# Attention and two MLPs on one core: tiles at multiples of 64 bytes, another rhythm of weight conversion, and the last cosine chunk in alternation with the last product

## The chip, the core and the metric

The kernel runs on one core of a Trainium2 chip. The metric is the device time of one execution in microseconds. The kernel before took 1944.91 us, the median of 3 runs (1944.83 to 1947.69).

## What is computed

All inputs are float32 or float64 arrays; the weights come as 64-bit words, which the kernel itself turns into float32.

```python
def _attn_ref(q, k, v):                        # (8, 8, 576, 64) each
    k_p = k.reshape(B, H, Sp, pool, D).mean(axis=3)      # pool = 8: 72 keys
    v_p = v.reshape(B, H, Sp, pool, D).mean(axis=3)
    scores = scale * np.matmul(q, k_p.transpose(0, 1, 3, 2))
    attn = softmax(scores)
    return np.matmul(attn, v_p)
...
x = attn_out.transpose(0, 2, 1, 3).reshape(4608, 512)
x = (sigmoid(x @ w_gate) * (x @ w_val)) @ w_out          # w_gate, w_val 512 x 1536, w_out 1536 x 512
h = x @ w_in                                             # 512 x 2048
out = (h * np.cos(h)) @ w2_out                           # 2048 x 512
```

## The kernel before

**Tiling.** The 4608 tokens make 9 chunks (`NC`) of 512 columns, kept transposed: a tile holds 128 features in its partitions and 512 tokens along them. Each product is made of three: an operand is split into a high part in float32r and the rest, and high x high, high x rest and rest x high are added up in a PSUM bank. So a block of 128 output features over 512 inputs takes 12 matmuls of 128x512 (`group` in what follows): 4 blocks of the contraction, 3 matmuls each. The last product, `y_step`, has the tokens as stationary and the weights as moving operand, and its groups have 12 matmuls too (4 token tiles, 3 each).

**Stages.** First, attention of chunk c + 1 runs beside the gate and value products of chunk c (`gv_step`, 12 pairs of groups `pg`, `pv` a chunk); the gated result goes to DRAM (`gd`). Chunk 8 has no attention beside it; there, from pair 3 on, one group of the product with `w_out` of chunk 0 (`o_step`, `po`) follows each pair, and the three that are left follow the last pair. Then come the cosine products: for each chunk 16 groups `ph` (`h_step`), with the 12 `po` groups of the next chunk between them. One group `ph` with what goes with it is called a turn here. Its cosine takes three operations of VectorE (`n`, `r`, `r`, L485 to L491), two of ScalarE (Sin, Square), and a fourth of VectorE (`rest`, L498), which is held back by one turn; `r` goes to DRAM (`hd`). At last, `y_step` runs 16 groups for each chunk, with `hd` fetched again.

**Order.** The program stands in the order in which it is written; each engine takes its instructions in that order. `o_ahead` and `y_ahead` fetch up to four tiles ahead on SyncE's queue and make the two parts of the next two (`parts`: a cast on ScalarE, a subtraction on VectorE, L66). Of the three matmuls of each contraction block, the first needs the cast and the second the subtraction.

**Weights.** A block of weights is 512 KB. `load_all` fills slots of 4096 bytes a partition; a block's raw words stand two slots ahead of where its parts go. There are 28 slots at first; slots come free as `w_gate`, `w_val` and `w_out` are used for the last time, and six more (`e0` to `e5`) with the pool `hp_`, when the gate stage's tiles are given up. `split` converts in three stages, for two blocks a call: `stage_exponent` (ScalarE, up to four blocks ahead), `stage_bits` (VectorE, two operations a block, L132 and L137), `stage_parts` (cast and subtraction). In chunks 0, 7 and 8 of the cosine products each turn calls `split`; the blocks of `w2_out` from the fifth on are loaded in chunk 7, each as a `w_out` block comes free.

**Banks.** PSUM has 8 banks in two sets of four, `t` and `g`. `pg`, `pv` and `ph` use `g`, attention and `po` use `t`, and chunk c of `y_step` uses `g` for even c, `t` for odd. A `ph` can only start once the `rest` of the fourth one before it is done.

**Addresses.** In the kernel as built, the pool of weights begins at byte 1152 of a partition and every slot in it, as every tile of `mp` behind it (`x2`, `fetch`, `parts`), begins at a multiple of 64. `mask` takes 32 bytes; all of attention's tiles after it begin 32 bytes past a multiple of 64. So does what is laid out from the top of memory, which ends at 229344: the gate stage's `xT` (186336 and 202720) and later `e0` to `e5` (184288 to 208864), where blocks 0 to 5 of `w2_out` end up. The moving operand of the gate stage's matmuls is `xT`, that of `y_step` is the block of `w2_out`, that of `po` and `ph` stands in `mp`.

Of the kernel before, what the change touches and what calls it, by code (L numbers as in the profile page):

```python
# [9 lines left out]
F32 = mybir.dt.float32  # L10
# [13 lines left out]
def attention_two_mlps(  # L24
# [22 lines left out]
    nc = tc.nc  # L47
    B, H, S, D = q.shape
    NT, DM = out.shape
    FF = w_gate.shape[1]  # L50
    FF2 = w2_in.shape[1]
    P = 128
# [5 lines left out]
    NF = FF // P  # L58
    NF2 = FF2 // P
    C = 512  # L60
    NC = NT // C
# [8 lines left out]
    dp = ctx.enter_context(tc.tile_pool(name="dp", bufs=1, space=bass.MemoryType.DRAM))  # L70
    ps = ctx.enter_context(tc.tile_pool(name="ps", bufs=1, space=bass.MemoryType.PSUM))
    at = tc.alloc_tile_pool(name="at", bufs=1, side="left")
    gv = tc.alloc_tile_pool(name="gv", bufs=1, side="right")

    gd = [dp.tile([NF, P, C], F32, name=f"gd{c}") for c in range(NC)]
# [2 lines left out]
    def bank(tag, shape, name):  # L78
        return ps.tile(shape, F32, tag=tag, name=name, bufs=4)
# [18 lines left out]
    slots = [(wp, f"w{n}") for n in range(NSLOT)]  # L98
# [43 lines left out]
    def stage_parts(n):  # L142
        (kind, f), (pool, tag) = order[n], slots[n]
        t = pool.tile([P, 2, 512], F32R, tag=tag, name=f"w{kind}{f}")
        x = words(n, F32, 1)
        nc.scalar.copy(t[:, 0], x)  # L146
        split_lo(nc.vector, t[:, 1], x, t[:, 0])
        blocks[kind, f] = t
        place[kind, f] = slots[n]

    def split(upto=None):

        upto = len(raws) if upto is None else upto
        while done["parts"] < done["bits"]:
            stage_parts(done["parts"])
            done["parts"] += 1
        while done["exponent"] < min(done["bits"] + 4, upto):
            stage_exponent(done["exponent"])
            done["exponent"] += 1
        some = range(done["bits"], min(done["bits"] + 2, done["exponent"]))  # L160
        stage_bits(some)
        done["bits"] += len(some)
# [7 lines left out]


    ident = at.tile([P, P], F32, name="ident")
    mask = at.tile([P, H], F32, name="mask")
    kbds = [at.tile([P, NP, 2 * KEYS], F32, name=f"kbd{n}") for n in range(2)]
    vm = at.tile([P, 2, NP, P], F32R, name="vm")
    vr = at.tile([P, 2, NP, P], F32R, name="vr")
# [274 lines left out]
    graw, gp, po = {}, {}, {}  # L451
# [52 lines left out]
    def y_step(c, j, g):  # L504
        w = block("o2", j)
        wh, wl = w[:, 0], w[:, 1]
        if j == 0:
            po[c] = [bank("gt"[c % 2], [P, DM], f"py{c}_{n}") for n in range(4)]
        for n in range(4):
            p = po[c][n]  # L510
            s = slice(n * P, (n + 1) * P)
            nc.tensor.matmul(p, g[:, 0, s], wh, start=j == 0, stop=False)  # L512
            nc.tensor.matmul(p, g[:, 0, s], wl, start=False, stop=False)  # L513
            nc.tensor.matmul(p, g[:, 1, s], wh, start=False, stop=j == NF2 - 1)  # L514
            if j == NF2 - 1:
                y = hp_.tile([P, DM], F32, tag="y", name=f"y{c}_{n}", bufs=4)
                if n % 2:
                    nc.scalar.mul(y, p, -1.0)
                else:
                    nc.vector.tensor_scalar(  # L520
                        out=y, in0=p, scalar1=-1.0, scalar2=None, op0=ALU.mult
                    )
                nc.sync.dma_start(out[c * C + n * P:c * C + (n + 1) * P, :], y)

    with tc.manual_schedule():
# [38 lines left out]
        at_o = {"fetched": 0, "split": 0, "next": 0}  # L564

        def o_ahead():
            while at_o["fetched"] < min(at_o["next"] + 4, len(osteps)):
                c, f = osteps[at_o["fetched"]]
                graw[c, f] = fetch(gd, c, f, "graw")
                at_o["fetched"] += 1  # L570
            while at_o["split"] < min(at_o["next"] + 2, len(osteps)):
                g_parts(*osteps[at_o["split"]])
                at_o["split"] += 1

        def o_next():
            c, f = osteps[at_o["next"]]
            o_step(c, f)
            at_o["next"] += 1
            if c == NC - 1:
                slots.append(place["o", f])  # L580
                load_all()

        store = None
        for c in range(NC):
            last = c == NC - 1
            beside = [] if last else plan(c + 1)
            if last:
                at.release()
                mp = tc.alloc_tile_pool(name="mp", bufs=1, side="left", reuse_waits="tile")
            for f in range(NF):  # L590
                if last and f >= 2:
                    o_ahead()
                done_ = gv_step(c, f)
                if c == 0:
                    split()
                    for _ in range(2):
                        if len(raws) < len(slots) - AHEAD:
                            load()
                if last:
                    slots.extend(place[kind, f] for kind in "gv")  # L600
                    load_all()
                    split(len(raws) - 2)
                    if f >= 3:
                        o_next()
                elif f % 4 == 3:
                    split()
                if beside:
                    for step in beside[f]:
                        step()
                if store:  # L610
                    store()
                store = done_
# [2 lines left out]

        gv.release()
        hp_ = tc.alloc_tile_pool(name="hp", bufs=1, side="right", reuse_waits="tile")
        slots.extend((hp_, f"e{n}") for n in range(6))
        load_all()
        while at_o["next"] < NF:  # L620
            o_ahead()
            o_next()
            split()

        ys = [(c, j) for c in range(NC) for j in range(NF2)]
        hraw, hp = {}, {}
        at_y = {"fetched": 0, "split": 0}

        def y_ahead(n):
            while at_y["fetched"] < min(n + 4, len(ys)):  # L630
                c, j = ys[at_y["fetched"]]
                hraw[c, j] = fetch(hd, c, j, "hraw")
                at_y["fetched"] += 1
            while at_y["split"] < min(n + 2, len(ys)):
                c, j = ys[at_y["split"]]
                hp[c, j] = parts(hraw.pop((c, j)), f"hp{c}_{j}")
                at_y["split"] += 1

        late = []
        for c in range(NC):  # L640
            for j in range(NF2):
                if c + 1 < NC:
                    o_ahead()
                elif j >= NF:
                    y_ahead(0)
                late.append(h_step(c, j))
                if len(late) > 1:
                    late.pop(0)()
                if c + 1 < NC and j < NF:
                    o_next()  # L650
                if c == 0 or c >= NC - 2:
                    split()
        for fn in late:
            fn()


        for n, (c, j) in enumerate(ys):
            y_ahead(n + 1)
            y_step(c, j, hp.pop((c, j)))
        mp.release()  # L660
        hp_.release()

# [31 lines left out]
```

## Time and profile before

| | |
|---|---|
| median of 3 runs | 1944.91 us |
| the profiled execution | 1945.53 us |
| its span | 1943.8 us |
| TensorE busy | 1863.7 us (96%) |
| VectorE, ScalarE busy | 1018.2 us (52%), 705.4 us (36%) |
| granted clock of TensorE, mean of the span | 0.982 |

The span runs from the first to the last instruction. A matmul of 512 columns is shown with some 0.39 us, though the next one starts earlier: the pitch is read from the starts. The timeline gives start, duration, engine, line, operation and tiles of each instruction and, in brackets, how long its engine had been idle and what ended that. Lines beginning with SPq are issues of DMAs by SyncE.

### The profile page before, as it was taken

How to read it: one execution, taken by the hardware profiler on the slowest of the kernel's cores; microseconds unless marked ns; L12 is line 12 of the kernel's file. 1: busy time of each engine (PE TensorE's matmuls, PEld its weight loads, DVE VectorE, ACT ScalarE, POOL GpSimd, SP SyncE). 2: the span in 40 equal slices, each digit the busy share in tenths (PEclk: the TensorE clock that was granted, in tenths of full speed). 3: DMA queues.
4: the chain of work that ended last, by engine and by line, in shares of the span. 5: the costliest groups of instructions: out<-in, count | busy, mean ns of one | idle time of the engine just before them, and what ended most of it. 6: DMA issues, size and time to landing. Idle time of an engine off the chain costs nothing.

```text
span 1943.8 us, 22603 instructions
## 1 busy us (share of the span) xinstructions
PE 1863.7 (96%) x8384; PEld 1518.7 (78%) x8384; DVE 1018.2 (52%) x1849; ACT 705.4 (36%) x1201; POOL 104.4 (5%) x149
## 2 busy tenths in 40 slices
PE   4899999999999999989999999999878899999999
PEld 3678888888888788878888888888756688888887
DVE  7784353434434344577676676776657722222222
ACT  3563343434334333444333333333334422222222
POOL 3202112021110000000000000000000000000000
PEclk7999999999999999999999999999988999999999
DMA  9533224142241116632322222223332333333333
GB/s 237 173 97 93 80 70 112 42 113 74 77 109 41 55 38 201 194 136 98 99 97 97 98 98 98 97 98 98 105 117 87 133 117 120 115 119 120 114 108 109
DMA packets 151470, 208.06 MB, mean 107 GB/s; under 512 B 48448, under 2 KB 68928, under 8 KB 151360
## 3 DMA queue, kind: packets, MB, share of 16 engines
q1 hardware_dynamic: 151360, 206.62, 34.6%
q8 instruction: 66, 1.08, 0.2%
q14 instruction: 44, 0.36, 0.1%
HBM read 131.07 MB, written 75.50 MB: 106 GB/s over the span
## 4 chain that ended last, share of the span: by engine, by line
PE 85%; DVE 7%; DMA 3%; ACT 2%; issue 1%; SPq 1%; ACTq 0%; DVEq 0%
PE py L514 7%; PE py L512 7%; PE py L513 7%; PE ph L481 5%; PE ph L480 5%; PE ph L482 5%; PE pg L384 5%; PE pg L386 5%; PE pg L385 5%; PE pv L386 5%; PE pv L384 5%; PE pv L385 5%; PE po L467 4%; PE po L466 4%; PE po L468 4%; PE px L371 3%
## 5 line engine op out<-in xcount | busy, mean ns | idle before, releaser
L391 DVE TENSOR_TENSOR g<-pv,s 128x512 f32<-128x512 f32 x108 | 74.6, 691 | 329.8 <-PE pv L386 204.9
L480 PE MATMUL ph<-x,wi 128*128 128x512 f32 x576 | 226.5, 393 | 11.8 <-DVE r L498 11.1
L66 DVE TENSOR_TENSOR hp<-hraw,hp 128x512 fp32r<-128x512 f32 x144 | 98.8, 692 | 259.1 <-ACT hp L442 258.9
L494 ACT ACTIVATE r<-r 128x512 f32<-128x512 f32 x144 | 91.1, 632 | 394.8 <-DVE r L491 394.8
L512 PE MATMUL py<-wo,hp 128*128 128x512 f32 x576 | 225.3, 391 | 1.9 <-DVE r L498 1.9
L481 PE MATMUL ph<-x,wi 128*128 128x512 f32 x576 | 225.9, 392 | 0.3 <-DVE x L66 0.3
L514 PE MATMUL py<-wo,hp 128*128 128x512 f32 x576 | 226.1, 392 | 0.0
L482 PE MATMUL ph<-x,wi 128*128 128x512 f32 x576 | 225.5, 391 | 0.0
L513 PE MATMUL py<-wo,hp 128*128 128x512 f32 x576 | 225.4, 391 | 0.0
L466 PE MATMUL po<-gp,wo 128*128 128x512 f32 x432 | 172.5, 399 | 20.5 <-ACT gp L442 20.5
L442 ACT CAST hp<-hraw 128x512 fp32r<-128x512 f32 x144 | 88.6, 621 | 258.2 <-PE py L514 232.1
L384 PE MATMUL pg<-xT,wg 128*128 128x512 f32 x432 | 179.0, 414 | 0.4 <-ACT wg L146 0.4
L467 PE MATMUL po<-gp,wo 128*128 128x512 f32 x432 | 173.6, 402 | 2.8 <-DVE gp L66 2.8
L386 PE MATMUL pg<-xT,wg 128*128 128x512 f32 x432 | 171.8, 398 | 0.5 <-DVE wg L66 0.4
L385 PE MATMUL pg<-xT,wg 128*128 128x512 f32 x432 | 171.5, 397 | 0.0
L468 PE MATMUL po<-gp,wo 128*128 128x512 f32 x432 | 171.4, 397 | 0.0
L386 PE MATMUL pv<-xT,wv 128*128 128x512 f32 x432 | 170.8, 395 | 0.0
L384 PE MATMUL pv<-xT,wv 128*128 128x512 f32 x432 | 170.7, 395 | 0.0
L385 PE MATMUL pv<-xT,wv 128*128 128x512 f32 x432 | 170.3, 394 | 0.0
L480 PEld LDWEIGHTS ph<-x,wi 128*128 128x128 f32 x576 | 109.0, 189 | 36.6 <-DVE r L498 12.4
L389 ACT ACTIVATE s<-pg 128x512 f32<-128x512 f32 x108 | 64.6, 598 | 190.5 <-PE pg L386 190.1
L66 DVE TENSOR_TENSOR gp<-graw,gp 128x512 fp32r<-128x512 f32 x108 | 74.5, 690 | 105.7 <-ACT gp L442 105.7
(108 smaller groups left out, 3027.2 us busy)
## 6 DMA issues: line engine op xcount, KB each, us to landing
hd<-r SPq DMA_DIRECT2D x144, 256.0 KB
hraw<-hd SPq DMA_DIRECT2D x144, 256.0 KB
gd<-g SPq DMA_DIRECT2D x108, 256.0 KB
graw<-gd SPq DMA_DIRECT2D x108, 256.0 KB
raw_o<-in_moe_w_out_dram SPq DMA_DIRECT2D x28, 512.0 KB
out_dram<-y SPq DMA_DIRECT2D x36, 256.0 KB
raw_k<-in_k_dram SPq DMA_DIRECT2D x32, 256.0 KB
q<-in_q_dram SPq DMA_DIRECT2D x32, 256.0 KB
```

Of the source, the lines that this page charges most:

```text
L384: nc.tensor.matmul(p, wh, x[:, 0, kb], start=kb == 0, stop=False)
L385: nc.tensor.matmul(p, wh, x[:, 1, kb], start=False, stop=False)
L386: nc.tensor.matmul(p, wl, x[:, 0, kb], start=False, stop=kb == KB - 1)
L466: nc.tensor.matmul(p, wh, g[:, 0], start=f == 0, stop=False)
L467: nc.tensor.matmul(p, wh, g[:, 1], start=False, stop=False)
L468: nc.tensor.matmul(p, wl, g[:, 0], start=False, stop=f == NF - 1)
L480: nc.tensor.matmul(p, wh, x[:, 0, kb], start=kb == 0, stop=False)
L481: nc.tensor.matmul(p, wh, x[:, 1, kb], start=False, stop=False)
L482: nc.tensor.matmul(p, wl, x[:, 0, kb], start=False, stop=kb == KB - 1)
L512: nc.tensor.matmul(p, g[:, 0, s], wh, start=j == 0, stop=False)
L513: nc.tensor.matmul(p, g[:, 0, s], wl, start=False, stop=False)
L514: nc.tensor.matmul(p, g[:, 1, s], wh, start=False, stop=j == NF2 - 1)
```

## The change

Four edits:

- **Addresses.** A tile of 32 bytes is allocated at the top of memory, and `mask` is widened to 64 bytes. As built, every operand of every matmul then begins at a multiple of 64: `xT` at 186304 and 202688, `e0` to `e9` at 176064 to 212928.
- **First products of chunk 0.** In the last gate chunk the pairs 3 to 10 are followed by 1, 1, 1, 2, 2, 2, 2 and 1 groups `po`, all twelve, and the loop behind the stage is gone. `hp_` brings ten slots in place of six, so that ten blocks (the last two of `w_in`, the first eight of `w2_out`) are loaded there at once. The output tile `y` shares four buffers with `r`.
- **Conversion.** In chunk 0 each turn calls `split` as before, in all others every third.
- **Last chunk.** In chunk 8 of the cosine products each turn ends with one group of the last product's chunk 0 and `y_ahead`; its first tiles are fetched from turn 12 of chunk 7 on. The last product's bank sets change places. Its other 8 chunks follow.

```diff
+    edge = ctx.enter_context(tc.tile_pool(name="edge", bufs=1, side="right"))
+    nc.gpsimd.memset(edge.tile([P, 8], F32, name="edge"), 0.0)
...
-    mask = at.tile([P, H], F32, name="mask")
+    mask = at.tile([P, 2 * H], F32, name="mask")[:, :H]
...
-            po[c] = [bank("gt"[c % 2], [P, DM], f"py{c}_{n}") for n in range(4)]
+            po[c] = [bank("tg"[c % 2], [P, DM], f"py{c}_{n}") for n in range(4)]
...
-                y = hp_.tile([P, DM], F32, tag="y", name=f"y{c}_{n}", bufs=4)
+                y = hp_.tile([P, DM], F32, tag="r", name=f"y{c}_{n}", bufs=4)
...
-                    if f >= 3:
+                    for n in range((0, 0, 0, 1, 1, 1, 2, 2, 2, 2, 1, 0)[f]):
+                        if n:
+                            o_ahead()
                         o_next()
...
-        slots.extend((hp_, f"e{n}") for n in range(6))
+        slots.extend((hp_, f"e{n}") for n in range(10))
         load_all()
-        while at_o["next"] < NF:
-            o_ahead()
-            o_next()
-            split()
...
             for j in range(NF2):
-                if c + 1 < NC:
+                if not last:
                     o_ahead()
-                elif j >= NF:
-                    y_ahead(0)
+                    if c == NC - 2 and j >= NF:
+                        y_ahead()
                 late.append(h_step(c, j))
                 if len(late) > 1:
                     late.pop(0)()
-                if c + 1 < NC and j < NF:
+                if last:
+                    y_next()
+                    y_ahead()
+                elif j < NF:
                     o_next()
-                if c == 0 or c >= NC - 2:
+                if c == 0 or j % 3 == 2:
                     split()
```

Three places show what moves (line numbers of the changed kernel are three higher from L73 on; `wi212` is block 12 of `w_in`, `raw_o28` the raw words of block 8 of `w2_out`, a digit pair such as `8_4` is chunk and block).

VectorE, turn 1 of chunk 0's cosine products, from its first operation to the next turn's. Before:

```order
L485 TENSOR_SCALAR n0_1_6918<-ph0_1_6905 128x512
L488 SCALAR_TENSOR_TENSOR r0_1_6919<-n0_1_6918,ph0_1_6905 128x512
L491 SCALAR_TENSOR_TENSOR r0_1_6919<-n0_1_6918,r0_1_6919 128x512
L498 SCALAR_TENSOR_TENSOR r0_0_6867<-r0_0_6867,ph0_0_6853 128x512
L66 TENSOR_TENSOR wo22_6939<-raw_o22_6747,wo22_6939 128x512
L66 TENSOR_TENSOR wo23_6942<-raw_o23_6749,wo23_6942 128x512
L66 TENSOR_TENSOR gp1_3_6947<-graw1_3_6848,gp1_3_6947 128x512
L485 TENSOR_SCALAR n0_2_6963<-ph0_2_6950 128x512
```

With the change:

```order
L488 TENSOR_SCALAR n0_1_6897<-ph0_1_6884 128x512
L491 SCALAR_TENSOR_TENSOR r0_1_6898<-n0_1_6897,ph0_1_6884 128x512
L494 SCALAR_TENSOR_TENSOR r0_1_6898<-n0_1_6897,r0_1_6898 128x512
L501 SCALAR_TENSOR_TENSOR r0_0_6842<-r0_0_6842,ph0_0_6828 128x512
L66 TENSOR_TENSOR wi212_6918<-raw_i212_6786,wi212_6918 128x512
L66 TENSOR_TENSOR wi213_6921<-raw_i213_6788,wi213_6921 128x512
L135 TENSOR_SCALAR raw_i214_6808<-raw_i214_6808 128x512
L135 TENSOR_SCALAR raw_i215_6810<-raw_i215_6810 128x512
L140 SCALAR_TENSOR_TENSOR raw_i214_6808<-raw_i214_6808 128x512
L140 SCALAR_TENSOR_TENSOR raw_i215_6810<-raw_i215_6810 128x512
L66 TENSOR_TENSOR gp1_3_6932<-graw1_3_6751,gp1_3_6932 128x512
L488 TENSOR_SCALAR n0_2_6948<-ph0_2_6935 128x512
```

The four operations on raw words (two `TENSOR_SCALAR`, two of the second kind) now stand in this turn, and blocks of `w_in` are still being converted here; turns of this form go on up to turn 5, where before turn 1 is the last with conversions at all.

ScalarE, turn 2 of chunk 7 and what follows. Before:

```order
L494 ACTIVATE r7_2_10960<-r7_2_10960 128x512
L495 ACTIVATE r7_2_10960<-r7_2_10960 128x512
L146 CAST wo25_10982<-raw_o25_10933 128x512
L127 ACTIVATE raw_o26_10980<-raw_o26_10980 128x512
L442 CAST gp8_4_10990<-graw8_4_10894 128x512
L494 ACTIVATE r7_3_11007<-r7_3_11007 128x512
L495 ACTIVATE r7_3_11007<-r7_3_11007 128x512
L146 CAST wo26_11029<-raw_o26_10980 128x512
L127 ACTIVATE raw_o27_11027<-raw_o27_11027 128x512
L442 CAST gp8_5_11037<-graw8_5_10941 128x512
```

With the change:

```order
L497 ACTIVATE r7_2_10988<-r7_2_10988 128x512
L498 ACTIVATE r7_2_10988<-r7_2_10988 128x512
L130 ACTIVATE raw_o28_10926<-raw_o28_10926 128x512
L130 ACTIVATE raw_o29_10967<-raw_o29_10967 128x512
L130 ACTIVATE raw_o210_11008<-raw_o210_11008 128x512
L445 CAST gp8_4_11019<-graw8_4_10928 128x512
L497 ACTIVATE r7_3_11036<-r7_3_11036 128x512
L498 ACTIVATE r7_3_11036<-r7_3_11036 128x512
L445 CAST gp8_5_11060<-graw8_5_10969 128x512
```

Before, each turn has one cast and one exponent operation, the latter on the block loaded in the same turn. Now turn 2 has three exponent operations, the last of them on the block loaded in the same turn, and turns 3 and 4 have none.

VectorE, the last turn of chunk 8. Before:

```order
L485 TENSOR_SCALAR n8_15_11858<-ph8_15_11845 128x512
L488 SCALAR_TENSOR_TENSOR r8_15_11859<-n8_15_11858,ph8_15_11845 128x512
L491 SCALAR_TENSOR_TENSOR r8_15_11859<-n8_15_11858,r8_15_11859 128x512
L498 SCALAR_TENSOR_TENSOR r8_14_11837<-r8_14_11837,ph8_14_11823 128x512
L498 SCALAR_TENSOR_TENSOR r8_15_11859<-r8_15_11859,ph8_15_11845 128x512
L66 TENSOR_TENSOR hp0_2_11871<-hraw0_2_11769,hp0_2_11871 128x512
```

With the change:

```order
L488 TENSOR_SCALAR n8_15_12122<-ph8_15_12109 128x512
L491 SCALAR_TENSOR_TENSOR r8_15_12123<-n8_15_12122,ph8_15_12109 128x512
L494 SCALAR_TENSOR_TENSOR r8_15_12123<-n8_15_12122,r8_15_12123 128x512
L501 SCALAR_TENSOR_TENSOR r8_14_12084<-r8_14_12084,ph8_14_12070 128x512
L523 TENSOR_SCALAR y0_0_12134<-py0_0_11542 128x512
L523 TENSOR_SCALAR y0_2_12146<-py0_2_11544 128x512
L66 TENSOR_TENSOR hp1_1_12157<-hraw1_1_12065,hp1_1_12157 128x512
L501 SCALAR_TENSOR_TENSOR r8_15_12123<-r8_15_12123,ph8_15_12109 128x512
```

The `rest` of the last cosine product (the last row) now stands behind two output tiles and a part of the last product's chunk 1, whose cast follows on ScalarE behind the output tiles `y0_1` and `y0_3`. As built, `y0_3` is given the buffer of `y0_0`, and the four banks of the last product's chunk 1 are those of `ph8_12` to `ph8_15` in this order.

## Rows read from the trace of the kernel before

**Rows 1.** The page: busy time of TensorE over the span; the granted clock in 40 slices; the engines' shares of the chain that ended last.

```profile
PE 1863.7 (96%) x8384; PEld 1518.7 (78%) x8384; DVE 1018.2 (52%) x1849; ACT 705.4 (36%) x1201; POOL 104.4 (5%) x149
...
PEclk7999999999999999999999999999988999999999
...
PE 85%; DVE 7%; DMA 3%; ACT 2%; issue 1%; SPq 1%; ACTq 0%; DVEq 0%
```

**Rows 2.** The view of windows, one line for each stretch: length, then busy time and number of instructions of each engine, the granted clock, the DMA share. The stretches run from the end of the last gate product to the second group of chunk 1's first products, on to chunk 7's third `po` group, on to the first cosine product of chunk 8, on to the second block of the last product, and to the end.

```profile
821.19:842.86 21.67, 16.34 (x61) 12.30 (x60) 15.20 (x28) 11.83 (x22) 0.00 (x0) 0.92 0.75 263
842.86:1386.87 544.01, 544.01 (x2402) 450.41 (x2400) 379.95 (x580) 204.64 (x347) 0.00 (x0) 1.00 0.29 96
1386.87:1490.75 103.88, 77.76 (x277) 57.27 (x276) 62.16 (x101) 36.29 (x62) 0.00 (x0) 0.89 0.30 104
1490.75:1546.30 55.55, 49.65 (x204) 39.89 (x205) 49.28 (x77) 25.61 (x41) 0.00 (x0) 0.94 0.30 109
1546.30:1943.80 397.50, 393.82 (x1717) 321.95 (x1715) 108.96 (x159) 96.15 (x158) 0.00 (x0) 1.00 0.37 117
```

**Rows 3.** The timeline of TensorE in the last gate chunk: the first matmul of the chunk, and the first `po` matmul, which follows on 96 gate matmuls.

```profile
731.80 0.39 PE L384 MATMUL pg<-xT,wg 128*128 128x512 f32 x1
...
754.20 0.39 PE L466 MATMUL po<-gp,wo 128*128 128x512 f32 x1
```

**Rows 4.** The timeline of TensorE: a cosine product's first matmul and the first of the `po` group behind it, 12 matmuls on; then chunk 3 of the last product, the first matmuls of its block 0, of its block 6 and of chunk 4's block 0 (72 and 120 matmuls on).

```profile
899.99 0.39 PE L480 MATMUL ph<-x,wi 128*128 128x512 f32 x1
...
902.71 0.39 PE L466 MATMUL po<-gp,wo 128*128 128x512 f32 x1
...
1675.64 0.40 PE L512 MATMUL py<-wo,hp 128*128 128x512 f32 x1
...
1692.45 0.40 PE L512 MATMUL py<-wo,hp 128*128 128x512 f32 x1
...
1719.69 0.40 PE L512 MATMUL py<-wo,hp 128*128 128x512 f32 x1
```

**Rows 5.** The timeline of TensorE: first matmuls of two `px` products of 5 matmuls each.

```profile
721.62 0.39 PE L371 MATMUL px<-aT,vm 128*128 128x512 f32 x1
...
722.76 0.39 PE L371 MATMUL px<-aT,vm 128*128 128x512 f32 x1
```

**Rows 6.** The timeline of VectorE behind the last gate group, which gives way to the next group's first matmul at 821.19 (the start of the first stretch of rows 2): the gated result, and the first operation behind the conversion of two blocks that follows.

```profile
821.44 0.69 DVE L391 TENSOR_TENSOR g<-pv,s 128x512 f32<-128x512 f32 x1 [4.01 <-ACT raw_i L127]
...
825.13 0.69 DVE L66 TENSOR_TENSOR gp<-graw,gp 128x512 fp32r<-128x512 f32 x1
```

**Rows 7.** The timeline of VectorE in chunk 0 of the cosine products: the first operation (`n<-ph`) of four turns running, and the subtraction `gp` ahead of the second. Conversions of two blocks lie in the first turn (operations on raw words and parts), in the second (parts alone) and not in the third.

```profile
845.57 0.68 DVE L485 TENSOR_SCALAR n<-ph 128x512 int32<-128x512 f32 x1
...
852.69 0.69 DVE L66 TENSOR_TENSOR gp<-graw,gp 128x512 fp32r<-128x512 f32 x1
853.29 0.69 DVE L485 TENSOR_SCALAR n<-ph 128x512 int32<-128x512 f32 x1
...
859.13 0.68 DVE L485 TENSOR_SCALAR n<-ph 128x512 int32<-128x512 f32 x1
...
863.75 0.68 DVE L485 TENSOR_SCALAR n<-ph 128x512 int32<-128x512 f32 x1
```

**Rows 8.** The timeline of ScalarE at the same place, its two longest waits for DMAs; in brackets the idle time before, and what ended it.

```profile
830.93 0.67 ACT L127 ACTIVATE raw_i<-raw_i 128x512 f32<-128x512 f32 x1 [3.87 <-DMA raw_i<-in_moe_w_in_dram]
...
838.24 0.62 ACT L442 CAST gp<-graw 128x512 fp32r<-128x512 f32 x1 [2.40 <-DMA graw<-gd]
```

**Rows 9.** The timelines of SyncE's queue and of ScalarE in chunk 7: the issue of a block's load, the exponent operation that waited for it, the cast behind that, and the next turn's load.

```profile
1390.11 0.38 SPq L115 DMA_DIRECT2D raw_o<-in_moe_w_out_dram  x1
...
1393.79 0.68 ACT L127 ACTIVATE raw_o<-raw_o 128x512 f32<-128x512 f32 x1 [2.85 <-DMA raw_o<-in_moe_w_out_dram]
1394.36 0.61 ACT L442 CAST gp<-graw 128x512 fp32r<-128x512 f32 x1
...
1398.88 0.38 SPq L115 DMA_DIRECT2D raw_o<-in_moe_w_out_dram  x1
```

**Rows 10.** The timelines of SyncE's queue, ScalarE and TensorE in chunk 8: the issue of the first loads of `hd`, the cast that waited for them, and the cosine product that started late.

```profile
1528.11 1.83 SPq L448 DMA_DIRECT2D hraw<-hd  x4
...
1530.96 0.62 ACT L442 CAST hp<-hraw 128x512 fp32r<-128x512 f32 x1 [2.57 <-DMA hraw<-hd]
...
1535.85 0.80 PE L480 MATMUL ph<-x,wi 128*128 128x512 f32 x1 [4.00 <-DVE r L498]
```

**Rows 11.** The view of windows around that product.

```profile
1535.85:1539.00 3.15, 3.15 (x8) 2.48 (x8) 3.08 (x5) 1.73 (x4) 0.00 (x0) 0.50 0.23 86
1539.00:1541.00 2.00, 2.00 (x6) 1.62 (x5) 1.93 (x4) 0.64 (x2) 0.00 (x0) 0.52 0.35 131
```

**Rows 12.** The timelines of VectorE (the four subtractions of a chunk's `x`; the last step `L491` of a cosine reduction, and `L498`) and of ScalarE (Sin; Square takes as long).

```profile
1479.09 2.48 DVE L66 TENSOR_TENSOR x<-po,x 128x512 fp32r<-128x512 f32 x4 [1.24 <-ACT x L470]
...
1539.79 0.69 DVE L491 SCALAR_TENSOR_TENSOR r<-n,r 128x512 f32<-128x512 int32 x1
1540.40 0.68 DVE L498 SCALAR_TENSOR_TENSOR r<-r,ph 128x512 f32<-128x512 f32 x1
...
1540.52 0.63 ACT L494 ACTIVATE r<-r 128x512 f32<-128x512 f32 x1 [1.36 <-DVE r L491]
```

More of the change, by code (lines that the diff above doesn't have):

```diff
@@ L617, in attention_two_mlps, with y_ahead @@
         hp_ = tc.alloc_tile_pool(name="hp", bufs=1, side="right", reuse_waits="tile")
-        slots.extend((hp_, f"e{n}") for n in range(6))
+        slots.extend((hp_, f"e{n}") for n in range(10))
         load_all()
-        while at_o["next"] < NF:
-            o_ahead()
-            o_next()
-            split()
         ys = [(c, j) for c in range(NC) for j in range(NF2)]
         hraw, hp = {}, {}
-        at_y = {"fetched": 0, "split": 0}
-        def y_ahead(n):
-            while at_y["fetched"] < min(n + 4, len(ys)):
+        at_y = {"fetched": 0, "split": 0, "next": 0}
+        def y_ahead():
+            while at_y["fetched"] < min(at_y["next"] + 4, len(ys)):
                 c, j = ys[at_y["fetched"]]
@@ L633, in y_ahead @@
                 at_y["fetched"] += 1
-            while at_y["split"] < min(n + 2, len(ys)):
+            while at_y["split"] < min(at_y["next"] + 2, len(ys)):
                 c, j = ys[at_y["split"]]
@@ L637, in y_ahead, with y_next @@
                 at_y["split"] += 1
+        def y_next():
+            c, j = ys[at_y["next"]]
+            at_y["next"] += 1
+            y_step(c, j, hp.pop((c, j)))
         late = []
         for c in range(NC):
+            last = c == NC - 1
             for j in range(NF2):
-                if c + 1 < NC:
+                if not last:
                     o_ahead()
-                elif j >= NF:
-                    y_ahead(0)
+                    if c == NC - 2 and j >= NF:
+                        y_ahead()
                 late.append(h_step(c, j))
@@ L654, in attention_two_mlps @@
             fn()
-        for n, (c, j) in enumerate(ys):
-            y_ahead(n + 1)
-            y_step(c, j, hp.pop((c, j)))
+        while at_y["next"] < len(ys):
+            y_next()
+            y_ahead()
         mp.release()
```

## The prediction

> **What bounds the kernel now.** I read the page first: TensorE is busy for 1863.7 of 1943.8 us and holds 85% of the chain that ended last, and its granted clock is full but for the start and a few slices around 1380 to 1540 us [rows 1]. So the time is TensorE's pitch times its matmuls, plus the places where it waits. Busy time doesn't tell the pitch; the starts do. In the cosine stage 12 matmuls of 512 columns take 902.71 - 899.99 = 2.72 us, 227 ns each [rows 4]. In the gate stage 96 take 754.20 - 731.80 = 22.40, 233.3 ns each [rows 3]. The last product shows both: blocks 0 to 5 take 16.81 us for 72 matmuls (233.5 ns), blocks 6 to 15 take 27.24 for 120 (227.0) [rows 4].
>
> Then the windows [rows 2]. At 2.72 us a group:
> - 821.19 to 842.86 holds 4 `po` and 1 `ph`, 13.6 us of work in 21.7: 8.1 lost.
> - 842.86 to 1386.87 is TensorE without a gap.
> - 1386.87 to 1490.75 (chunk 7) holds 10 `po` and 13 `ph`, 62.6 in 103.9: 41.3 lost.
> - 1490.75 to 1546.30 (chunk 8) holds 16 `ph` and one block of the last product, 46.2 in 55.6: 9.3 lost.
>
> These four things, 58.7 us of waits and the slow pitch, are what the change touches. The sum is made against the profiled execution, 1945.53 us; the median of the runs is 0.6 lower.
>
> **Addresses.** The slow pitch is found exactly where the moving operand begins 32 bytes past a multiple of 64: `xT`, and the slots `e0` to `e5`. The same lines of the last product, with the same stationary operand, run at 227 ns as soon as the block stands in a slot at a multiple of 64 [rows 4]. I take the address as the cause. Gate stage: 2592 matmuls x (233.3 - 227.0) = 16.4 us. Last product: 9 chunks x (16.81 - 72 x 0.227 = 0.47) = 4.2 us. Together **20.6 us**. Both lie on TensorE's own path, with nothing to hide them. Of attention's matmuls, five of 512 columns take 722.76 - 721.62 = 1.14 us [rows 5], 228 ns, though both of their operands begin 32 past: an offset that the two share costs little, it seems. I put nothing for them, nor for the tile's one memset.
>
> The Trainium skill (SBUF — State Buffer, Specifications) gives 16-byte cachelines and a penalty for crossing to a new one. 32 and 0 past a multiple of 64 both begin such a line, so by that this edit gives nothing; the rows differ by 6 ns a matmul all the same. With a gain of nothing the sum would end 20.6 us higher.
>
> **The first products of chunk 0.** The 12 `po` groups are the same work; inside the gate stage, where TensorE doesn't wait, they cost their pitch. What goes is the 8.1 us: ScalarE stood 3.9 us for a raw block and 2.4 for `graw`, with the cast for the next `po` behind that [rows 8].
>
> In its place comes a loop. When the gate stage ends, blocks 10 to 15 of `w_in` still want parts, and eight blocks of `w2_out` follow; so turns 0 to 5 of chunk 0 hold both kinds of VectorE work on two blocks each. In a turn VectorE reduces `ph`, ScalarE does Sin, Square and two casts, VectorE subtracts, works on the raw words, then makes the `gp` part for the next `po`. The trace has one such turn: 853.29 - 845.57 = **7.72 us**; with parts alone 859.13 - 853.29 = 5.84; with none 863.75 - 859.13 = 4.62 [rows 7]. TensorE needs 5.44 for a turn. Count from the end of the last gate group. VectorE is through with the gated result and two blocks at 3.9 (825.13 - 821.19) [rows 6], so the first reduction starts at 4.1. Turn 0 has four exponent operations and waits for two of them: 8.3, next reduction at 12.4. Turns 1 to 5 bring it to 51.0, turn 6 to 56.8. `po` group k needs its part at 5.44k + 2.72 and has it when reduction k - 1 starts: 12.4 for 13.6 (k = 2), 51.0 for 40.8 (k = 7), 56.8 for 46.2 (k = 8), from then on falling back. TensorE ends up **10.7 us** late. Ten blocks at once are 5.2 MB, 6.8 with two more and two stores ahead of them; at the 263 GB/s of the first stretch [rows 2] the fifth `graw` behind them lands 26 us in, when the loop reaches its cast: covered, or else 2 us more. Bounds: 4 (if part of the VectorE work overlaps) to 16.
>
> **Conversion in chunk 7.** Before, each turn is a ring: load (SyncE, when `po` frees the slot), exponent, cast for `gp`, VectorE, `po`; 1398.88 - 1390.11 = 8.77 us a turn, of which the load till the exponent takes 3.7 [rows 9]. Now only turns 2 and 5 wait for a block loaded in the same turn. Behind that exponent on ScalarE stand the cast of `gp` for the next turn's `po`, and then Sin and Square. In turn 2 the load goes out 6.7 us after the turn's start (behind a store), lands at 10.4, exponent, cast and part end at 12.4; `po` 4 needs it at 13.6. No wait, but VectorE is 4 us behind, and each plain turn gives back only 5.44 - 4.62 = 0.8. The same in turn 5 makes `po` 7 0.5 late; turn 8, a full one, 0.7. VectorE is still 1.6 behind at turn 11. There the `po` groups end and TensorE runs four `ph` in a row, 5.44 + 4 x 2.72 = 16.3 us, while VectorE has five turns of 2.8, the subtractions of `x` (2.5) [rows 12], two rounds of conversion (3.3 and 1.3) and two parts of `hraw` (1.5): 22.4. The four banks take up some; `ph` 15 needs the bank of `ph` 11, free at 17.6, and wants it at 13.6: 4.0 late. The loads of `hd` land while VectorE is still busy. Left of 41.3: 0.5 + 0.7 + 4.0 = **5.2 us**, with bounds of 1 and 12.
>
> **Chunk 8.** Before, it lost its 9.3 when `y_ahead` put casts ahead of Sin, 2.6 us for the DMA, with 4.0 on TensorE and the clock at half after it [rows 10, 11]. Now a turn is `ph` and one group of the last product, 5.44 us, and the loop has the form of a plain turn, 4.62 [rows 7]: covered by 0.8. In the last turn `rest` of `ph` 15 stands behind two output tiles and a part. From that turn's start: reduction ends at 5.0, the `rest` before it at 5.6, `y0_0` at 6.3; its store lands after some 2.8 (the nearest row, a load of that size: 1530.96 - 1528.11 [rows 10]) at 9.2; only then ScalarE may write `y0_3`, 9.9, then the cast, 10.6; VectorE's part, 11.3, `rest`, 12.0. The fourth bank of chunk 1 is wanted at 5.44 + 2.04 = 7.5. So 4.5 us of wait, and after a wait of 4.0 the trace has 12 matmuls in 5.2 us at half clock (1.2 GHz) [rows 11], 2.5 more: **7.0 us**, with bounds of 3 and 9.
>
> **Sum.** 1945.53 - 20.6 - 58.7 + 10.7 + 5.2 + 7.0 = 1889.1; on the median, 1888.5.
>
> **Rivals.**
> 1. *The waits go altogether.* The loop of rows 7 is read from a single turn, and the end from buffers that could come free earlier. With none of the 22.9 us left: 1866; with bounds of 4, 1 and 3 left, 1873.5. Against it: VectorE's order is fixed, and its work for turns 0 to 6, some 45 us, doesn't fit into 38.
> 2. *The address isn't the cause.* Slots `e0` to `e5` and `xT` share a second thing, the upper end of memory. The change leaves them there, and four more blocks join them: 1888.5 + 20.6 + 9 x 48 x 6.5 ns (2.8) = 1912; without such a place, if the 6 ns have some third cause that stays, 1909. For it: `px`, lower in memory, has the offset and not the price [rows 5]. Against it: among the matmuls of 512 columns, stationary and moving operand stand 32 apart (modulo 64) in all the slow ones and in none of the others, `px` included. The rule on lines in the Trainium skill (SBUF — State Buffer, Specifications) would have it end here too.
> 3. *Chunk 8 falls to half clock, and the result is slower than before.* If each of its turns made TensorE wait, the clock could drop as in rows 11 and stay: a turn of 24 matmuls then takes 10.4 in place of 5.44, 5 us more. It decides from 12 such turns on; all 16 give 1888.5 + 79 = 1968. Against it: a plain turn is 0.8 shorter than TensorE's, and after the waits of chunk 7, one a turn, the window's clock is still 0.89 [rows 2].
> 4. *The ring of chunk 7 comes back for turns 2 to 8*, as the exponents take what was loaded last: 7 x 3.3 = 23 more, 1906 to 1912.
>
> **Chances.** My forecast, with its bounds, 0.80; rival 1 0.07; rival 2 0.08; rival 4 0.03; rival 3 0.02. The terms' bounds make 1888.5 - 15 and + 14; I reach to 1905 since waits that I overlooked only add. Range 1873 to 1905. A measurement here tells 0.2% (some 4 us) from no change. Faster by more than that: 0.97; within: 0.01; slower: 0.02.
>
> **What would show it.** Right: 12 gate matmuls in 2.72 us; turns of 7.7 on VectorE in chunk 0 and some 11 us of TensorE's waits there, with `gp` as the cause; chunk 7 with waits of a few us near its end alone; chunk 8 without any until its last turn. Wrong: a gate stage at 233 ns; chunk 0 of the cosine products without waits; TensorE waiting for `raw_o` or `hp` in each turn of chunks 7 or 8.

## The result, and the profile after

The changed kernel takes **1901.1 us**, the median of 4 runs (1899.34 to 1902.48), against 1944.87 (1944.28 to 1947.69) of the kernel before in runs beside it: a ratio of 0.9772, 95% interval 0.9755 to 0.9789. The profiled execution took 1901.13 us, its span is 1899.4. The forecast was 1888.5 in a range of 1873 to 1905: the sign and the range held, the point lies 12.6 too low.

The page of the changed kernel, the lines that answer to [rows 1]:

```profile
PE 1842.1 (97%) x8384; PEld 1515.3 (80%) x8384; DVE 1016.6 (54%) x1849; ACT 702.7 (37%) x1201; POOL 105.0 (6%) x150
...
PEclk7999999999999899999999999999999999999999
...
PE 87%; DVE 7%; ACT 3%; issue 2%; DMA 1%; SPq 0%; ACTq 0%; DVEq 0%
```

TensorE's busy time fell by 21.6 us with as many matmuls: part of that is pitch, part is matmuls that no longer run at half clock. DMA has gone from 3% of the chain to 1%.

The view of windows of the changed kernel: gate chunk 8 with all `po` of chunk 0, cosine chunks 0, 1 to 6, 7, then 8 (with chunk 0 of the last product), chunk 1 of the last product, and the rest. Columns as in [rows 2].

```profile
724.30:823.36 99.06, 99.06 (x433) 81.11 (x432) 48.66 (x88) 39.78 (x72) 0.00 (x0) 1.00 0.59 192
823.36:912.12 88.76, 80.74 (x338) 63.69 (x336) 69.97 (x117) 41.44 (x72) 0.00 (x0) 0.98 0.41 145
912.12:1369.10 456.98, 456.98 (x2017) 378.38 (x2016) 317.65 (x482) 170.22 (x289) 0.00 (x0) 1.00 0.29 97
1369.10:1451.63 82.53, 78.35 (x338) 64.08 (x336) 63.99 (x104) 36.38 (x62) 0.00 (x0) 0.98 0.41 143
1451.63:1539.62 87.99, 87.99 (x385) 72.08 (x384) 57.13 (x87) 30.59 (x52) 0.00 (x0) 1.00 0.29 96
1539.62:1588.60 48.98, 45.71 (x194) 37.10 (x192) 14.28 (x22) 12.33 (x21) 0.00 (x0) 0.97 0.38 120
1588.60:1899.40 310.80, 307.13 (x1345) 252.16 (x1343) 85.89 (x126) 76.50 (x126) 0.00 (x0) 1.00 0.37 119
```

Chunks 0 and 7 hold 28 groups each, 76.2 us at 2.72: they lose 88.8 - 76.2 = **12.6** and 82.5 - 76.2 = **6.4**. Chunk 8 has no gap. Chunk 1 of the last product holds 16 groups, 43.8 at the pitch of the chunk that follows: **5.1** lost. That is 24.1 of waits and of half clock behind them, where the forecast left 22.9.

*Pitch.* The timeline of TensorE in the last gate chunk, first matmul of the chunk and first `po`, 96 matmuls on (compare [rows 3]):

```profile
724.30 0.39 PE L387 MATMUL pg<-xT,wg 128*128 128x512 f32 x1
...
746.28 0.39 PE L469 MATMUL po<-gp,wo 128*128 128x512 f32 x1
```

21.98 us, 228.9 ns each; 233.3 before, 227 forecast. In the last product blocks 0 to 9, which all stand in `e` slots now, run at 229 too.

*Chunk 0.* The timeline of VectorE, first operations of four turns, and the view of waits of TensorE there (total, times, longest; us):

```profile
844.34 0.68 DVE L488 TENSOR_SCALAR n<-ph 128x512 int32<-128x512 f32 x1
...
852.06 0.68 DVE L488 TENSOR_SCALAR n<-ph 128x512 int32<-128x512 f32 x1
...
859.78 0.68 DVE L488 TENSOR_SCALAR n<-ph 128x512 int32<-128x512 f32 x1
...
867.50 0.68 DVE L488 TENSOR_SCALAR n<-ph 128x512 int32<-128x512 f32 x1
```

```profile
PE po L470 <- DVE gp L66: 5.6, 5, 1.9
PE po L469 <- ACT gp L445: 1.5, 3, 0.6
PE ph L483 <- DVE r L501: 0.8, 1, 0.8
```

A full turn is 7.72 us to the hundredth, as read from the single one before [rows 7]; `gp` is what TensorE waits for. Behind the third of these stops it also ran at half clock, by the view of windows:

```profile
860.44:863.85 3.41, 3.41 (x9) 2.68 (x9) 2.04 (x5) 1.87 (x4) 0.00 (x0) 0.50 0.14 53
```

By the starts of the matmuls the stops for `gp` cost 9.7 us in all, the half clock 1.6 and the wait for `rest` 1.1. (The view of waits counts from the end that a matmul is shown with, 0.39 us behind its start, so each stop costs more than it says.)

*End of chunk 8.* The timelines of VectorE, ScalarE and SyncE in the last turn, in order of time; the turn starts at 1534.18.

```profile
1539.16 0.68 DVE L501 SCALAR_TENSOR_TENSOR r<-r,ph 128x512 f32<-128x512 f32 x1
...
1539.76 0.68 DVE L523 TENSOR_SCALAR y<-py 128x512 f32<-128x512 f32 x1
...
1540.47 3.15 SPq L526 DMA_DIRECT2D out_dram<-y  x4
...
1542.66 0.60 ACT L521 ACTIVATE y<-py 128x512 f32<-128x512 f32 x1 [1.60 <-DMA out_dram<-y]
1543.16 1.13 ACT L445 CAST hp<-hraw 128x512 fp32r<-128x512 f32 x2
...
1543.80 0.69 DVE L66 TENSOR_TENSOR hp<-hraw,hp 128x512 fp32r<-128x512 f32 x1 [1.10 <-ACT hp L445]
1544.41 0.68 DVE L501 SCALAR_TENSOR_TENSOR r<-r,ph 128x512 f32<-128x512 f32 x1
```

The forecast's chain, link by link: output tile, its store, `y0_3` on ScalarE behind that store, cast, part, `rest`. `rest` is done 10.9 us into the turn (forecast 12.0), mostly since the store took 2.2, not 2.8.

### The profile page after: what moved, and what is told of

Same layout as the page of the kernel before. It is cut to its first block, busy times and chain, and to the rows that moved or that the text cites. A ratio compares the mean times of both kernels' runs of the same rounds, so it can differ in the third digit from the quotient of the medians.

```text
span 1899.4 us, 22583 instructions
## 1 busy us (share of the span) xinstructions
PE 1842.1 (97%) x8384; PEld 1515.3 (80%) x8384; DVE 1016.6 (54%) x1849; ACT 702.7 (37%) x1201; POOL 105.0 (6%) x150
## 4 chain that ended last, share of the span: by engine, by line
PE 87%; DVE 7%; ACT 3%; issue 2%; DMA 1%; SPq 0%; ACTq 0%; DVEq 0%
PE py L515 7%; PE py L517 7%; PE py L516 7%; PE ph L483 6%; PE ph L485 6%; PE ph L484 6%; PE pg L387 5%; PE pg L389 5%; PE pg L388 5%; PE pv L389 5%; PE pv L387 5%; PE pv L388 5%; PE po L470 4%; PE po L471 4%; PE po L469 4%; PE px L374 3%
## 5 line engine op out<-in xcount | busy, mean ns | idle before, releaser
L470 PE MATMUL po<-gp,wo 128*128 128x512 f32 x432 | 169.5, 392 | 5.7 <-DVE gp L66 5.6
L469 PE MATMUL po<-gp,wo 128*128 128x512 f32 x432 | 169.4, 392 | 1.5 <-ACT gp L445 1.5
L471 PE MATMUL po<-gp,wo 128*128 128x512 f32 x432 | 168.8, 391 | 0.0
```

The costliest lines, as they stand in the source:

```text
L469: nc.tensor.matmul(p, wh, g[:, 0], start=f == 0, stop=False)
L470: nc.tensor.matmul(p, wh, g[:, 1], start=False, stop=False)
L471: nc.tensor.matmul(p, wl, g[:, 0], start=False, stop=f == NF - 1)
```

## The experiments

Times are medians; each ratio is to the kernel before, run on the same chip beside it (1945.4 to 1947.0). Edits are to the changed kernel unless said otherwise.

### The two halves

`addr_only` is the kernel before with these two edits alone, `order_only` the changed kernel without them:

```diff
+    nc.gpsimd.memset(edge.tile([P, 8], F32, name="edge"), 0.0)
...
-    mask = at.tile([P, H], F32, name="mask")
+    mask = at.tile([P, 2 * H], F32, name="mask")[:, :H]
```

> The kernel before with the two address edits alone. In the changed kernel 12 gate matmuls take 2.75 us, before they took 2.80, and 2.72 was forecast. Theory A (the pitch follows how far moving and stationary operand stand apart modulo 128 bytes: 96 apart 233 ns, 64 apart 229, nothing 227): gate groups at 2.75, blocks 0 to 5 of the last product 2.75 in place of 2.80; some 2592 x 4.3 ns + 648 x 4.5 ns = 14 us less, 1931 us. Theory B (32 bytes past a multiple of 64 cost 4.5 ns, and the upper end of memory 2.3 ns by itself): the same here. Theory C (the gate stage hides half of the gain behind other engines): gate groups at 2.72 wherever nothing waits.

> The changed kernel without the two address edits, so that xT and the ten slots lie 32 bytes past a multiple of 64 again. The rest of the change is worth what its windows show: 58.7 us of waits became some 24, so 34 us less than before, 1911 us, if the parts simply add up; gate groups at 2.80 and blocks 0 to 9 of the last product at 2.80. If the schedule's waits depend on the pitch, the sum with the other half will miss the whole change by several us.

`addr_only` 1933.49, 0.9939 (0.9925 to 0.9954); `order_only` 1915.96, 0.9847 (0.9831 to 0.9864). So addresses give 12.2 us, the order 29.7, together 41.9; the whole gives 1944.87 - 1901.1 = 43.8. The 1.9 between lies within the intervals (some 3 us each way), but there is an account for it: with ten `e` slots in place of six, blocks 6 to 9 move to the slower side, 9 x 48 matmuls, at 6.6 ns more each in `order_only` (2.8 us) and 2.2 in the whole (1.0). That an address edit alone gains shows the address as a cause. It gains 12, not 20.6. `order_only` ended 5 above its expectation, which took the addresses to be worth 10 there; they are worth 43.8 - 29.7 = 14.

### What about the addresses

```diff
-    nc.gpsimd.memset(edge.tile([P, 8], F32, name="edge"), 0.0)
+    nc.gpsimd.memset(edge.tile([P, 24], F32, name="edge"), 0.0)
```

This is `edge96`: 96 bytes at the top of memory. With 16 columns (64 bytes) it is `off32`, with 56 (224) `off128`; `align128` has the 96 bytes, and the small tiles of attention widened so that every tile begins at a multiple of 128. `left64` keeps the 32 bytes and adds 64 ahead of the weights' slots:

```diff
+    nc.gpsimd.memset(wp.tile([P, 16], F32, name="shift"), 0.0)
```

> The changed kernel with every tile at a multiple of 128 bytes (edge 96 bytes, mask 128, mx and sm 64 each), at the same end of memory. Theory A: gate groups fall from 2.75 to 2.72 us, blocks 0 to 9 of the last product from 2.75 to 2.72, px from 1.14 to 1.135 for five matmuls; 2592 x 2.3 + 1080 x 2.3 ns = 8.5 us less, 1892 to 1893 us. Theory B (upper end of memory): nothing changes, 1901 us, 2.75.

> The changed kernel with all tiles of the lower side (weights' slots, x2, parts, attention) moved up by 64 bytes; those of the upper side stay. xT, e0 to e9 and the slots then all lie 64 past a multiple of 128. Theory A (only the distance between the two operands counts): gate groups and blocks 0 to 9 of the last product at 2.72, po and ph stay at 2.72; 1892 to 1893 us. Theory D (each operand by itself wants a multiple of 128): gate groups at 2.75 or slower, and po, ph and the last product's other blocks rise from 2.72 to 2.75, some 4000 x 2.3 ns = 9 us more, 1910 us. Theory B (upper end of memory): as the changed kernel, 1901 us.

> The changed kernel with an edge of 224 bytes: xT and the ten slots lie at a multiple of 256, the lower side's slots 128 past one, so that moving and stationary operand stand 128 apart in the gate stage and in blocks 0 to 9 of the last product. Theory A as it stands (modulo 128): gate groups at 2.72, as with nothing apart, 1895 us. Theory A2 (the distance counts modulo 256, since attention's px, 128 apart in one of the runs, went from 229 to 232 ns): gate groups at 2.79 or slower, 1908 to 1914 us.

> The changed kernel with a tile of 96 bytes at the top of memory in place of 32, and nothing else: every moving operand of 512 columns then stands at a distance of 0 (modulo 256) from its stationary operand, but for px, which stays at 64. Theory (the distance modulo 256 sets the pitch): gate groups at 2.72 us in place of 2.75, blocks 0 to 9 of the last product at 227 ns in place of 229, px at 229 as it is: 2592 x 2.3 ns + 1080 x 2.3 ns = 8.4 us less, 1892.5 us. Rival (the slower start of the two kernels before with a distance of 0, 4 us of low clock, belongs to this distance): 1896.5 us. Rival (only tiles at multiples of 128 bytes from the bottom of memory gain): no change, 1901.

> The changed kernel with a tile of 64 bytes at the top in place of 32: the moving operands of the gate stage and of blocks 0 to 9 of the last product begin at an odd multiple of 32 again, 32 bytes from their stationary operands (modulo 256). Theory (the pitch rises with the distance modulo 256: 0 gives 227 ns, 64 gives 229, 96 and 128 give 233.5): about 228 ns, 1896 to 1897 us. Rival (the prediction's own reading: operands 32 apart modulo 64 are the slow ones): 233.5 ns in the gate stage and in blocks 0 to 9, 1901 + 10 + 4.5 = 1915 us.

Measured: `align128` 1897.09, 0.9753 (0.9738 to 0.9767); `left64` 1896.87, 0.9749 (0.9734 to 0.9763); `off128` 1912.54, 0.9825 (0.981 to 0.984); `edge96` 1892.81, 0.9727 (0.9713 to 0.9742); `off32` 1915.58, 0.9844 (0.9828 to 0.986). The timelines of TensorE, of `edge96`, `off32` and `left64` (lines one higher) from the first gate matmul of chunk 8 to the first `po`, of `off128` from block 0 of a chunk of the last product to block 6 and to block 10:

```profile
719.63 0.39 PE L387 MATMUL pg<-xT,wg 128*128 128x512 f32 x1
...
741.39 0.39 PE L469 MATMUL po<-gp,wo 128*128 128x512 f32 x1
```

```profile
731.27 0.40 PE L387 MATMUL pg<-xT,wg 128*128 128x512 f32 x1
...
753.67 0.39 PE L469 MATMUL po<-gp,wo 128*128 128x512 f32 x1
```

```profile
724.05 0.39 PE L388 MATMUL pg<-xT,wg 128*128 128x512 f32 x1
...
745.81 0.39 PE L470 MATMUL po<-gp,wo 128*128 128x512 f32 x1
```

```profile
1643.05 0.40 PE L515 MATMUL py<-wo,hp 128*128 128x512 f32 x1
...
1659.84 0.40 PE L515 MATMUL py<-wo,hp 128*128 128x512 f32 x1
...
1671.04 0.39 PE L515 MATMUL py<-wo,hp 128*128 128x512 f32 x1
```

| distance of the moving operand's address from the stationary one's, modulo 256 | pitch | kernel |
|---|---|---|
| 0 | 21.76 / 96 = 226.7 ns | `edge96` |
| 32 | 22.40 / 96 = 233.3 ns | `off32` |
| 64 | 21.98 / 96 = 228.9 ns | changed kernel |
| 96 | 22.40 / 96 = 233.3 ns | before [rows 3] |
| 128 | 16.79 / 72 = 233.2 ns (last product; 22.31 / 96 = 232.4 in the gate stage) | `off128` |

In `left64` all operands of the gate stage begin at 64 past a multiple of 128 and their pitch is 21.76 / 96 = 226.7 ns: not each operand's own address counts but the distance between the two. `off128` sorts out what modulus: a distance of 128 costs in full, so it isn't 128. Nor is it above 256: in `edge96` the operands of the gate stage stand an odd multiple of 256 apart (`xT` at 186240, the slots from 1152 on in steps of 4096), those of `po` and `ph`, as built, a multiple of 512, and both run at 227. `off32` overturned the theory that I had by then, that the pitch grows with the distance: 32 costs as much as 96. What stands is that an equal offset modulo 256 is fast, 64 costs 2.2 ns and 32, 96 and 128 cost 6 to 6.6; distances above 128 were not tried. `px` fits: 64 apart in the kernel before, 228 ns [rows 5].

By whole times `align128` and `left64` are not clear of the changed kernel (0.9755 to 0.9789); their pitch is. They got 4 us less than it promised: their first gate product starts at 54.1 and 53.2 us (49.8 in the changed kernel); from 20 to 60 us the granted clock is 0.62 and 0.66 there (0.70), the DMA share 0.67 in both (0.83). `edge96`, with the same distance of 0, starts at 48.7 and gains 8.3 of 8.4 expected (1.1 of them by that earlier start), so the distance is not the reason. What in the other two slows the start stays open.

### The waits

```diff
 spread:
-                if c == 0 or j % 3 == 2:
+                if j % 3 == 2:
 shift7:
+                if c == 0 or (j % 3 == 2 and (c != NC - 2 or j < 9)):
 flush, in the last chunk ahead of y_next():
+                    if j == NF2 - 1:
+                        late.pop(0)()
```

> The changed kernel with a conversion in every third turn of chunk 0 too, as in the other chunks. In the changed kernel chunk 0's cosine stage takes 88.8 us for 28 groups (76.2 at 2.72), 12.6 lost. Theory of the loop (a turn with both kinds of conversion lasts 7.7 us on VectorE and ScalarE, a plain one 4.6, TensorE needs 5.4): three turns take 17.0 for 16.3, so chunk 0 loses 0 to 4 us, and the whole takes 1890 us. Rival (chunk 0 is late because ten blocks are loaded at once, and graw behind them): the loads are the same, so the 12.6 us stay, 1901 us.

> The changed kernel with the rest of the last cosine product put right behind its reduction, ahead of the last product's output tiles. In the changed kernel the first block of the last product's chunk 1 waits 3.3 us for it, and the second runs at half clock, 5.2 us in all over 2 groups. Theory (VectorE stands behind a cast that stands behind an output tile, whose buffer waits for a store): the wait and the half clock go, 1896 us. Rival (the bank is late for the reduction itself, 5.0 us behind the start of the turn, and Sin and Square): a wait of 1 to 3 us stays and with it the clock, 1899 us or more.

> The changed kernel with the conversions of chunk 7's turns 11 and 14 moved into turns 2 and 5 of chunk 8. In the changed kernel chunk 7 loses 6.4 us, 4.3 of them in a wait for the rest of product 11, and the rest in the half clock behind it. Theory (VectorE has 22 us of work for the last 16 us of TensorE's): 4.6 us less work there, the wait falls to 0 to 2 us, chunk 8 takes the two full turns in its stride (5.4 a turn against 7.7 once and 4.6 otherwise), 1896 us. Rival (ScalarE's casts stand behind the first loads of hd, as in the kernel before): the wait stays near 4 us, 1901 us.

The intervals of these three overlap that of the changed kernel (0.9755 to 0.9789): what they show is read from single chunks, not from the whole time. A chunk that an edit doesn't touch varies too: with the instructions of the changed kernel, chunk 7 takes 82.3 to 85.2 us and chunk 1 of the last product 47.9 to 50.5 in the traces of this case. The clock behind a wait is what differs. The wait for `rest` ahead of that chunk 1 is 3.2 to 3.3 us long in all of them; half clock behind it lasted 3.4 us in the changed kernel and 6.8 in `spread`, and in `off32` there was none.

`spread` 1899.53, 0.9756 (0.9742 to 0.9771): a miss, 1890 was expected. TensorE's waits in its cosine chunks and the turn to the last product, to be read against those of chunk 0 above:

```profile
PE ph L483 <- DVE r L501: 9.0, 2, 4.8
PE py L515 <- DVE r L501: 3.3, 1, 3.3
PE po L469 <- ACT gp L445: 0.8, 1, 0.8
PE po L470 <- DVE gp L66: 0.6, 2, 0.3
```

The waits for `gp` in chunk 0 are gone (what is left of them stands in chunk 7), which shows the full turns as their cause. But conversions now stand in turns 11 and 14, where four cosine products follow each other, and chunk 0 gets the end that chunk 7 has: a wait for `rest`, and half clock behind it. Chunk 0 still loses 7.5, and of the 5.1 gained there 2.7 went in chunk 7, which the edit leaves as it was:

```profile
823.20:906.90 83.70, 78.89 (x337) 64.77 (x336) 64.93 (x106) 37.98 (x65) 0.00 (x0) 0.96 0.45 157
...
1364.10:1449.30 85.20, 79.72 (x337) 64.60 (x336) 64.78 (x105) 36.96 (x63) 0.00 (x0) 0.96 0.40 138
```

`shift7` 1897.38, 0.9746 (0.9732 to 0.9761): chunk 7 takes 79.8 us, 2.7 less than in the changed kernel and 2.5 less than in any trace here with those conversions. The clock is full, and the wait at its end is 1.4 in place of 4.2:

```profile
1369.60:1449.40 79.80, 77.33 (x337) 62.83 (x336) 59.56 (x96) 34.97 (x60) 0.00 (x0) 1.00 0.42 144
```

So the conversions in its turns 11 and 14 make most of that wait, not the subtractions of `x` alone.

`flush` 1899.53, 0.9757 (0.9741 to 0.9773), where 1896 was expected: chunk 1 of the last product takes 46.4, 2.6 less, with the clock full. The wait for `rest` is gone; the view of waits has a new one in its place, so half of the loss stays:

```profile
PE py L515 <- ACT hp L445: 2.0, 1, 2.0
```

The cast still stands behind `y0_3`, which waits for a store, now that of the last cosine product, whose buffer it is given.

### Together

```diff
-                if c == 0 or j % 3 == 2:
+                if j % 3 == 2 and (j < 9 or last):
...
                 if last:
+                    if j == NF2 - 1:
+                        late.pop(0)()
+                        at_y["next"] += 1
+                        y_ahead()
+                        at_y["next"] -= 1
                     y_next()
```

`turns` has these two edits, `turns_edge96` the 96 bytes of `edge96` as well.

> The changed kernel with conversions in turns 2, 5 and 8 alone in chunks 0 to 7 (chunk 8 as it was), and in the last turn of chunk 8 the held-back step of the cosine product and the parts of the last product's chunk 1 ahead of the four output tiles. Theory (each wait that is left comes from VectorE's work in the turn, and from the order in that last turn): chunk 0 loses 1 to 4 us in place of 12.6 (three turns of 7.7, 4.6 and 4.6 against 16.3 of TensorE, then a ring of four cosine products at its end), chunk 7 loses 3.7 in place of 6.4, the place behind chunk 8 under 1.5 in place of 5.1: 1901 - 10 - 2.7 - 4 = 1884 us. Rival (a wait that is taken away comes back later, as in the kernels that changed one of these places): one of the three keeps its loss at half clock, 1890 us or more.

> Both of the former: the 96 bytes at the top, the conversions in turns 2, 5 and 8, the other order in the last turn. Theory: the two add up, 1884 - 8.4 = 1876 us, 0.964 of the kernel before. Rival (faster matmuls leave VectorE less time, and part of the gain goes into waits): 1880 to 1884 us.

`turns` 1885.06, 0.9689 (0.9673 to 0.9705); `turns_edge96` **1876.2**, 0.9640 (0.9626 to 0.9654), which beats both kernels. The view of windows of `turns`: cosine chunks 0, 1 to 6, 7, 8, and chunk 1 of the last product.

```profile
823.10:901.30 78.20, 76.51 (x337) 62.98 (x336) 59.52 (x97) 34.70 (x60) 0.00 (x0) 1.00 0.47 164
901.30:1359.70 458.40, 457.25 (x2017) 378.30 (x2016) 327.06 (x502) 176.94 (x301) 0.00 (x0) 1.00 0.29 97
1359.70:1440.40 80.70, 77.41 (x338) 62.87 (x338) 59.66 (x96) 35.01 (x60) 0.00 (x0) 1.00 0.41 143
1440.40:1528.40 88.00, 88.00 (x386) 72.06 (x385) 61.38 (x95) 32.22 (x55) 0.00 (x0) 1.00 0.31 99
1528.40:1572.20 43.80, 43.80 (x193) 36.02 (x192) 14.03 (x22) 12.30 (x21) 0.00 (x0) 1.00 0.42 134
```

Lost in chunks 0, 7, 8 and that chunk 1: 2.0, 4.5, 0 and 0, in place of 12.6, 6.4, 0 and 5.1. No conversion is left out, but not all stay where they were: the parts of all eight `w2_out` blocks, and the work on the raw words of six, go from chunk 0 into chunks 1 and 2. That costs one wait for `rest`, 1.15 us in chunk 1; chunks 1 to 6 take 458.4 in place of 457.0.

## Why the prediction was right, and where it was not

- **The four lost places (58.7 us).** Right. The time between the same points of both kernels shows it (before, after; us): ninth gate chunk and cosine chunk 0, from 731.80 to 916.3 and from 724.30 to 912.12, 184.5 and 187.8; chunks 1 to 6, 457.0 and 457.0; chunk 7, 117.5 and 82.5; from chunk 8 to the last product's chunk 1, 96.8 and 88.0; that chunk, 44.1 and 49.0.
- **The loop of chunk 0 (10.7).** Measured 12.6. The stops for `gp`, which the count is about, cost 9.7. The half clock behind the third of them (1.6) and a wait for `rest` near the chunk's end (1.1) were left out: that the total comes near is in part luck. `spread` and `turns` show the cause of the stops as argued.
- **Chunk 7 (5.2).** Measured 6.4. `ph7_15` waited 4.2 for the bank, forecast 4.0. The 0.5 and 0.7 of turns 5 and 8 didn't come; the half clock behind the wait, left out here, did: 10 matmuls in 3.4 us, first line below. `shift7` shows that conversions made most of the wait.
- **The end of chunk 8 (7.0).** Measured 5.1: mechanism as forecast, the wait 3.3 in place of 4.5, and half clock for 3.4 us (second line). `flush` and `turns` show that it is the order of instructions there.

The view of windows of the changed kernel, behind `ph7_15`'s start and behind that of the last product's fourth bank:

```profile
1447.50:1450.90 3.40, 3.40 (x10) 2.64 (x8) 3.30 (x6) 1.61 (x3) 0.00 (x0) 0.51 0.30 111
...
1546.50:1549.90 3.40, 3.40 (x10) 2.62 (x9) 1.39 (x2) 1.17 (x2) 0.00 (x0) 0.50 0.96 314
```

- **Addresses (20.6).** This term was mis-sized, and it is 10.0 of the 12.6. From the first gate product to the ninth gate chunk the kernels take 731.80 - 50.5 = 681.3 and 724.30 - 49.8 = 674.5, 6.8 less; the ninth chunk's own pairs 3 x 0.42 = 1.3; the last product 0.2 a chunk, 1.8; the start 0.7 (not the addresses' doing: `order_only`, without these edits, starts at 49.4): 10.6 in all. The step that failed is "as soon as the block stands in a slot at a multiple of 64": those slots stand at the same offset modulo 256 as the stationary operand, and the changed `xT` and `e` slots 64 away from it. So the new pitch is 229, not 227, and the four more blocks in `e` slots, which were counted in a rival only, lose by it. What was needed stood in the trace: `px`, 64 apart, showed 228 where 227 was the best, and I took that for costing little. By pitch alone the term is 8 x 288 x 4.4 ns = 10.1 for eight gate chunks, and 1.3 and 1.8 as above: 13.2, near what `addr_only` gained. That step made 7.4 of the miss. The 3.3 that the eight gate chunks gave less than 10.1 has another source: half of it is in the last of them (gate chunk 7), which took 81.4 in place of 80.9, with the clock at half for 10.2 us in place of 6.8. The others gave 0.8 to 1.2 each for 1.3; why not all of it stays open. That the range held is luck as far as this term goes: it had no bounds of its own, and the range's upper end had been stretched for waits.
- **The sum with measured terms:** 1945.53 - 10.6 - 58.7 + 12.6 + 6.4 + 5.1 = 1900.3, against 1901.13.
- **Rivals.** Rival 1 (waits go): no. Rival 2 (the address isn't the cause): no, `addr_only` alone gains 12.2; what spoke against it there, operands 32 apart modulo 64, was the better reading than the absolute address, and `off32` bears it out as far as it goes (128 is slow too). The rule of the Trainium skill (SBUF — State Buffer, Specifications) that was weighed with it, lines of 16 bytes, would have it end without a gain. The runs don't bear that out: all operands of the table begin at multiples of 32, and the pitches differ by 6.6 ns. Rivals 3 and 4 did not happen: chunk 8 has a clock of 1.00, and in chunk 7 the view of waits has a single one, 4.2 at its end.

## What to carry to other kernels

Before aligning operands, read the pitch from starts for each pair of operands and compare the offset of the two against each other modulo 256, not each one's alignment. Work on an engine that is not the bottleneck is best put where that engine's turn is shorter than the bottleneck's: the same conversions cost 12.6 us in consecutive turns of chunk 0 and 3.4 in every third turn of chunks 0 to 2 (2.0 and 1.4), but in a stretch without slack they only move the wait (`spread`). Of a short wait, ask what stands in the queue behind it: at the end of chunk 8, taking away one wait uncovered the next, and only moving both removed the loss. And the time of a whole kernel is a poor measure of one short wait: the half clock behind other waits varied by as much as these edits gained.

## What the runs showed of the hardware

- The pitch of these matmuls (512 columns, fp32r) depends on the distance between their operands' addresses: 226.7 ns at 0, 228.9 at 64, 232.4 to 233.3 at 32, 96 and 128 (modulo 256).
- Behind waits of 4.2 and 3.3 us TensorE ran at 1.2 GHz (granted clock 0.51 and 0.50) for 3.4 us; in `turns`, whose longest wait in these stretches is 2.3 us, the clock stayed at 1.00. The length of a wait alone doesn't decide it: behind the wait of 3.2 us at the same place in `off32` the clock stayed at 1.00, and in chunk 0 of the changed kernel it fell to 0.50 for 3.4 us behind three stops in 18 us, none with a wait above 1.1.
